# Leaky relu as one parametric relu on ScalarE, and the low weight parts of layers 1 and 2 made on VectorE

## The chip, the cores and the metric

One core of a Trainium2 chip runs the whole program. The metric is the device time of the program in microseconds, lower being better. Its engines are TensorE (PE in the profile, PEld its weight loads), VectorE (DVE), ScalarE (ACT), GpSimd (POOL) and SyncE (SP, which issues the DMAs); 16 DMA engines move the data. Every engine works through its own instructions in the order in which they stand, and waits at the first one whose operands are not ready.

## The reference

A chunked attention over 4 batches of 768 tokens with 8 heads of 64, followed by two MLP blocks over the 3072 tokens, all in float32:

```
scores = scale * (q_c @ k_full.T); scores -= max; a = exp(scores); a /= (sum(a) + 1e-9)
attn   = a @ v_full                       # per chunk of 32 tokens, window of 64 keys
h = x @ w_in;  g = maximum(0.01 * h, h);  x = g @ w_out        # 512 -> 2048 -> 512
a = x @ w_a;   b = x @ w_b;   out = (a * b) @ w_out2           # 512 -> 1536 -> 512
```

## The kernel before

**Products.** A float32 product is made of three passes: each operand is split into a rounded high part (dtype float32r) and a low part, which is the operand minus its high part, and TensorE adds low times high, high times low and high times high. `w_parts` (L91 to L94) does the split of a weight: ScalarE copies it into the high part (L93), another engine subtracts (L94). `split_g` (L316 to L323) does the same for the hidden activations, with L320 on ScalarE and L321 on an engine that is handed in. `a_out` (L289, L290) does it for the output of attention.

**Weights.** They come in as 64 bit words with their halves apart (tile `raw`). For each of the 32 tiles of the first MLP (16 blocks `f` of w_in and 16 of w_out) ScalarE scales the upper half (L79), VectorE joins the two halves with three integer operations (L83, L86, L87) into a tile `z` (three buffers), and then `w_parts` makes the slot `w` that TensorE loads. `Weights.step` joins one tile and splits the one before it. Before the change L94 stands on GpSimd for these 32 tiles.

**Stages.** The tokens go in six blocks `bi` of 512. For each block and each `f`, `mm1` (L377) multiplies x by a block of w_in into a PSUM tile `h` (two buffers), makes the leaky relu and the split, and `mm2` (L388) multiplies the result by a block of w_out and adds into four PSUM tiles; `mm2` is issued two items behind `mm1` (LAG = 2). Block 0 runs while its weights are still being made, in half tiles of 256 tokens, and so has three more items. Beside the items of a block stands the attention of the next four units `u` of 128 tokens: scores on TensorE (L202), softmax on VectorE and ScalarE (L215 to L233, Exp on L220), 16 transposes of `p` into `pt` on VectorE (L246), and the product with v on TensorE (L276). In blocks 1 to 4 the weights of the second MLP are prepared as well (`prep_steps`: `pz`, `ps`, `pw`), their low parts on GpSimd; this part is not changed. After block 5 come layers 3 and 4 (L662 to L740).

**Order.** The kernel is written in one sequence; a scheduling layer then sets the order of each engine's instructions from its own estimate of their durations, so an edit of one instruction moves others too.

**The leaky relu before.** ScalarE makes `t` = 0.01 h out of PSUM (L383), VectorE takes the larger of `t` and `h` (L385), which gives `g`; ScalarE then makes `gh` (L320) and GpSimd (block 0) or VectorE (blocks 1 to 5) makes `gl` (L321). There are 99 such tiles: 93 of 512 columns, 6 of 256.

Of the kernel before, what the change touches and what calls it, by code (L numbers as in the profile page):

```python
# [7 lines left out]
F32 = mybir.dt.float32  # L8
F32R = mybir.dt.float32r
I32 = mybir.dt.int32  # L10
AF = mybir.ActivationFunctionType
ALU = mybir.AluOpType
AX = mybir.AxisListType

P = 128
# [11 lines left out]
TB = 512  # L27
# [4 lines left out]
def kernel(  # L32
# [10 lines left out]
    nc = tc.nc  # L43
# [11 lines left out]
    tp = ctx.enter_context(tc.tile_pool(name="tp", bufs=4, side="right"))  # L55
# [210 lines left out]
    def a_pv(u, pool, tag):  # L266
        pt = PT[u % 2]
        o = pool.tile([P, KC, UT], F32, tag=tag, name="pv")
        for cp in range(2):
            v = vt.pop((u, cp))  # L270
            for pair in range(2):
                for cpar in range(2):
                    for hpar in range(2):
                        i = ((cpar * 2 + hpar) * 2 + pair) * 64
                        t0 = (2 * cp + cpar) * CH
                        nc.tensor.matmul(  # L276
                            o[64 * hpar:64 * hpar + 64, 2 * pair:2 * pair + 2, t0:t0 + CH],
                            v[:, i:i + 64],
                            pt[:, 2 * cp + pair, 2 * cpar + hpar].rearrange("p h q -> p (h q)"),
                            start=True, stop=True,  # L280
                        )
        pvt[u] = o
# [3 lines left out]
    def a_out(u, blk, off):  # L286
        o = pvt.pop(u)
        hi, lo = x1[blk]
        nc.scalar.copy(hi[:, :, off:off + UT], o)  # L289
        nc.vector.tensor_tensor(  # L290
            out=lo[:, :, off:off + UT], in0=o, in1=hi[:, :, off:off + UT].bitcast(F32),
            op=ALU.subtract,
        )

    def x_tiles(key):
        hi = xp.tile([P, KC, TB], F32R, tag="xh", name="xh")
        lo = xp.tile([P, KC, TB], F32R, tag="xl", name="xl")
        x1[key] = (hi, lo)
# [8 lines left out]
    def proj(ps, slot, x, c):  # L307
        hi, lo = x
        for kc in range(KC):
            mm3(  # L310
                ps[:, c],
                (slot[:, 0, kc * P:kc * P + P], slot[:, 1, kc * P:kc * P + P]),
                (hi[:, kc, c], lo[:, kc, c]),
                kc == 0, kc == KC - 1,
            )

    def split_g(g, c, eng):
        gh = tp.tile([P, TB], F32R, tag="gh", name="gh", bufs=3)
        gl = tp.tile([P, TB], F32R, tag="gl", name="gl", bufs=3)
        nc.scalar.copy(gh[:, c], g[:, c])  # L320
        eng.tensor_tensor(  # L321
            out=gl[:, c], in0=g[:, c], in1=gh[:, c].bitcast(F32), op=ALU.subtract
        )  # L323
        return gh, gl
# [6 lines left out]
    W1 = Weights(order)  # L331
# [29 lines left out]
    v_load(6)  # L361
    a_turn_pe(1, ps_a, "a")
    a_out(0, ("x", 0), 0)
    W1.step(nc.gpsimd)
    a_pv(1, ps_h, "h")
    v_load(8)
    W1.load(8)
    W1.split(1, nc.gpsimd)
    a_out(1, ("x", 0), UT)
    a_scores(2)  # L370
    a_soft1(2)
# [5 lines left out]
    def mm1(bi, parts):  # L377
        ps = ps_h.tile([P, TB], F32, tag="h", name="h")
        for o, n, f in parts:
            proj(ps, wslot[f, 0], x1["x", bi], slice(o, o + n))  # L380
        c = slice(min(o for o, _, _ in parts), max(o + n for o, n, _ in parts))
        t = tp.tile([P, TB], F32, tag="t", name="t")
        nc.scalar.mul(t[:, c], ps[:, c], 0.01)  # L383
        g = tp.tile([P, TB], F32, tag="t", name="g")
        nc.vector.tensor_tensor(out=g[:, c], in0=t[:, c], in1=ps[:, c], op=ALU.max)  # L385
        return split_g(g, c, nc.gpsimd if bi == 0 else nc.vector)

    def mm2(bi, parts, g):  # L388
        if bi not in acc:
            acc[bi] = [ps_a.tile([P, TB], F32, tag="a", name="a") for _ in range(KC)]  # L390
        gh, gl = g
        for o, n, f in parts:
            slot = wslot[f, 1]
            t = slice(o, o + n)
            for e in range(KC):
                ps = acc[bi][e][:, t]
                c = slice(e * P, e * P + P)

                kw = dict(skip_group_check=n < TB)
                nc.tensor.matmul(  # L400
                    ps, slot[:, 1, c], gh[:, t], start=f == 0 and o == 0, stop=False, **kw
                )
                nc.tensor.matmul(ps, slot[:, 0, c], gl[:, t], start=False, stop=False, **kw)  # L403
                nc.tensor.matmul(  # L404
                    ps, slot[:, 0, c], gh[:, t], start=False, stop=f == NF1 - 1, **kw
                )
            if f == NF1 - 1:
                for e in range(KC):
                    ps = acc[bi][e][:, t]
                    y = tp.tile([P, TB], F32, tag="z", name="x2", bufs=3)  # L410
                    if e % 2:
                        nc.vector.tensor_copy(y[:, t], ps)  # L412
                    else:
                        nc.scalar.copy(y[:, t], ps)
                    nc.sync.dma_start(out=x2d[bi][:, e, t], in_=y[:, t])
# [114 lines left out]
    def xs_load(sb):  # L530
        for h, tag in enumerate(("xh", "xh" if sb else "xl")):
            t = xp.tile([P, KC, TB], F32, tag=tag, name="xs")
            nc.sync.dma_start(out=t, in_=x2d[2 * sb + h])
            xs[sb, h] = t
# [8 lines left out]
    def xc_make(sb, i):  # L543
        (b11, b21), (b12, b22) = [
            (xs[sb, h][:, 0:HC, :], xs[sb, h][:, HC:KC, :]) for h in range(2)
        ]

        def sub(x, y, key):
            t = xq.tile([P, HC, TB], F32, tag="tt", name="tt", bufs=2)
            nc.vector.tensor_tensor(out=t, in0=x, in1=y, op=ALU.subtract)  # L550
            tt[key] = t
            return t

        if i == 0:
            xc_parts(sb, 0, b11)
            sub(b12, b11, 1)
            sub(b22, tt[1], 2)
        elif i == 1:
            xc_parts(sb, 1, b21)
        elif i == 4:  # L560
            xc_parts(sb, 4, tt[2])
        elif i == 3:
            xc_parts(sb, 3, tt[1])
        elif i == 5:
            xc_parts(sb, 5, sub(b22, b12, 3))
        elif i == 2:
            t = tt[2]
            nc.vector.tensor_tensor(out=t, in0=b21, in1=t, op=ALU.subtract)
            xc_parts(sb, 2, t)
        else:  # L570
            xc_parts(sb, 6, b22)
# [8 lines left out]
    def wo_load(upto):  # L580
        while wo_next[0] < upto:
            b, f = 1 + wo_next[0] // NF1, wo_next[0] % NF1
            if b == NB3:
                break
            t = wop.tile([P, 2, 512], F32R, tag="wo", name="w")
            nc.sync.dma_start(out=t.bitcast(F32), in_=wod[f])
            wslot[f, 1] = t
            wo_next[0] += 1

    for n, (bi, f, parts) in enumerate(items):  # L590
        first, last = bi == 0, bi == NB3 - 1
        if last and f == 0:
            for _ in steps:
                pass
            att.__exit__(None, None, None)
            xq = ctx.enter_context(
                tc.tile_pool(name="xq", bufs=1, side="left", reuse_waits="tile")
            )
        if f == 0 and not last:
            x_tiles(("x", bi + 1))  # L600
        if first:
            W1.load(2 * f + 14)
            W1.step(nc.gpsimd)
        behind.append((bi, parts, mm1(bi, parts)))
        if first:
            W1.step(nc.gpsimd)
        if len(behind) > LAG:
            mm2(*behind.pop(0))
        for fn in beside.get((bi, f), []):
            fn()  # L610
        if not first:
            wo_load((bi - 1) * NF1 + f + 4)

            i = (bi - 1) * NF1 + f
            for _ in range(84 * (i + 1) // 64 - 84 * i // 64):
                next(steps, None)
        elif f >= NF1 - 1:
            wo_load(f - NF1 + 2)
        if last:
            if f == 2:  # L620
                xs_load(0)
            if 4 <= f < 11:
                xc_make(0, CHAIN[f - 4])
# [209 lines left out]
```

## Time and profile before

| | |
|---|---|
| median of 3 runs | 1226.71 us (1224.39 to 1227.79) |
| the profiled execution, its own time | 1226.21 us |
| its span, from the first to the last instruction | 1224.4 us |
| mean granted TensorE clock over the span | 0.982 of full speed |
| PE busy | 1170.7 us, 96% of the span |
| DVE busy | 752.9 us, 61% |
| ACT busy | 383.1 us, 31% |
| POOL busy | 145.4 us, 12% |

Busy shares are averages over stages that have different limits, so they are read together with a table by stage. What a busy engine costs is read from the waits of the engine that sets the end, which here is PE.

### The profile page before, as it was taken

The numbers are of one execution on the slowest core, as the hardware profiler recorded it, in microseconds if no ns is written. First come the engines' busy times: TensorE is split into PE (matmuls) and PEld (weight loads), VectorE is DVE, ScalarE is ACT, GpSimd is POOL, SyncE is SP. The second block draws the span as 40 slices with busy tenths as digits, with TensorE's granted clock in tenths as the row PEclk, the third lists the DMA queues.
The fourth block names the chain that finished last, engine by engine and source line by source line (L and its number), as shares of the span: only waits on it lengthen the run. The fifth ranks groups of instructions, "written<-read, shape, count | busy, mean of one in ns | idle before, by whom it ended". The sixth has DMA issues, their size and how long they took to land.

```text
span 1224.4 us, 16825 instructions
## 1 busy us (share of the span) xinstructions
PE 1170.7 (96%) x6632; PEld 984.1 (80%) x6632; DVE 752.9 (61%) x1313; ACT 383.1 (31%) x642; POOL 145.4 (12%) x109
## 2 busy tenths in 40 slices
PE   5788799989998999999999999999999999999998
PEld 5778788867887887888888888888888888888887
DVE  5999959795897899666622443447443447433443
ACT  3634333243334433222422222224122223222220
POOL 1544512032122222000000000000000000000000
PEclk9898999989999999999999999999999999999999
DMA  9766658768887887642633843537453535453512
GB/s 322 256 229 194 210 186 306 268 238 299 297 304 254 310 311 261 212 138 86 221 106 108 319 158 120 193 125 280 162 215 130 198 131 208 158 204 120 189 61 103
DMA packets 63822, 250.72 MB, mean 205 GB/s; under 512 B 7424, under 2 KB 8832, under 8 KB 56832
## 3 DMA queue, kind: packets, MB, share of 16 engines
q1 hardware_dynamic: 63744, 249.66, 57.5%
q8 instruction: 52, 0.85, 0.3%
q14 instruction: 26, 0.21, 0.1%
HBM read 200.34 MB, written 49.28 MB: 204 GB/s over the span
## 4 chain that ended last, share of the span: by engine, by line
PE 67%; DVE 2%; DMA 1%; issue 0%; POOL 0%; SPq 0%; DVEq 0%; POOLq 0%
PE o L729 5%; PE o L730 5%; PE o L731 5%; PE A L662 4%; PE A L663 4%; PE A L664 4%; PE h L303 4%; PE a L403 4%; PE a L404 4%; PE a L400 4%; PE h L304 3%; PE h L305 3%; PE C L662 3%; PE C L663 3%; PE C L664 3%; PE D L663 1%
## 5 line engine op out<-in xcount | busy, mean ns | idle before, releaser
L303 PE MATMUL h<-xh,w 128*128 128x512 f32 (+1 forms) x448 | 168.8, 377 | 17.5 <-POOL w L94 14.7
L400 PE MATMUL a<-gh,w 128*128 128x512 f32 (+1 forms) x448 | 161.3, 360 | 4.8 <-DVE x L412 2.3
L304 PE MATMUL h<-xl,w 128*128 128x512 f32 (+1 forms) x448 | 164.2, 367 | 0.5 <-DVE xl L290 0.5
L305 PE MATMUL h<-xh,w 128*128 128x512 f32 (+1 forms) x448 | 163.7, 365 | 0.0
L403 PE MATMUL a<-gl,w 128*128 128x512 f32 (+1 forms) x448 | 160.8, 359 | 0.0
L404 PE MATMUL a<-gh,w 128*128 128x512 f32 (+1 forms) x448 | 160.8, 359 | 0.0
L303 PEld LDWEIGHTS h<-xh,w 128*128 128x128 f32 x448 | 87.5, 195 | 33.2 <-POOL w L94 15.7
L729 PE MATMUL o<-w,cl 128*128 128x512 f32 x288 | 112.1, 389 | 0.2 <-DMA w<-wod 0.2
L730 PE MATMUL o<-w,ch 128*128 128x512 f32 x288 | 112.0, 389 | 0.0
L731 PE MATMUL o<-w,ch 128*128 128x512 f32 x288 | 112.0, 389 | 0.0
L385 DVE TENSOR_TENSOR g<-t,h 128x512 f32<-128x512 f32 (+1 forms) x99 | 66.1, 668 | 67.3 <-ACT t L383 66.5
L320 ACT CAST gh<-g 128x512 fp32r<-128x512 f32 (+1 forms) x99 | 60.1, 607 | 149.5 <-DVE g L385 144.1
L246 DVE STREAM_TRANSPOSE pt<-p 32x128 f32<-32x128 f32 x320 | 96.8, 302 | 5.5
L400 PEld LDWEIGHTS a<-gh,w 128*128 128x128 f32 x448 | 84.6, 189 | 18.6 <-DVE x L412 2.9
L304 PEld LDWEIGHTS h<-xl,w 128*128 128x128 f32 x448 | 87.7, 196 | 13.1 <-DVE xl L290 0.9
L305 PEld LDWEIGHTS h<-xh,w 128*128 128x128 f32 x448 | 87.0, 194 | 13.3
L404 PEld LDWEIGHTS a<-gh,w 128*128 128x128 f32 x448 | 84.7, 189 | 12.5
L403 PEld LDWEIGHTS a<-gl,w 128*128 128x128 f32 x448 | 84.6, 189 | 12.5
L383 ACT ACTIVATE t<-h 128x512 f32<-128x512 f32 (+1 forms) x99 | 57.5, 581 | 110.3 <-PE h L305 110.3
L684 DVE TENSOR_TENSOR ga<-u,C 128x512 f32<-128x512 f32 x36 | 24.8, 688 | 105.4 <-ACT u L676 76.2
L676 ACT COPY u<-A 128x512 f32<-128x512 f32 x72 | 42.3, 587 | 143.5 <-PE A L664 143.5
L662 PE MATMUL A<-ch,wab 128*128 128x512 f32 x216 | 84.1, 389 | 0.0
(95 smaller groups left out, 2116.3 us busy)
## 6 DMA issues: line engine op xcount, KB each, us to landing
wab<-wab SPq DMA_DIRECT2D x36, 1792.0 KB, 7.3
w<-wod SPq DMA_DIRECT2D x116, 512.0 KB, 4.7
raw<-w SPq DMA_DIRECT2D x68, 512.0 KB, 5.9
wab<-pw SPq DMA_DIRECT2D x12, 1792.0 KB, 6.7
k<-kl SPq DMA_DIRECT2D x48, 256.0 KB, 4.3
v<-vl SPq DMA_DIRECT2D x48, 256.0 KB, 4.7
wod<-w SPq DMA_DIRECT2D x16, 512.0 KB, 5.3
q<-ql SPq DMA_DIRECT2D x48, 128.0 KB, 4.1
```

What stands on the lines that cost most here:

```text
L246: nc.vector.transpose(out=pt[o0:o0 + 32, :, 2 * cpar + hpar, hpx, :], in_=p[i0:i0 + 32, hpx::2, 32 * b:32 * b + 32],)
L303: nc.tensor.matmul(ps, w[1], x[0], start=first, stop=False)
L304: nc.tensor.matmul(ps, w[0], x[1], start=False, stop=False)
L305: nc.tensor.matmul(ps, w[0], x[0], start=False, stop=last)
L400: nc.tensor.matmul(ps, slot[:, 1, c], gh[:, t], start=f == 0 and o == 0, stop=False, **kw)
L403: nc.tensor.matmul(ps, slot[:, 0, c], gl[:, t], start=False, stop=False, **kw)
L404: nc.tensor.matmul(ps, slot[:, 0, c], gh[:, t], start=False, stop=f == NF1 - 1, **kw)
L662: nc.tensor.matmul(ps, w[:, 1, i, c], hi[:, kc], start=first and kc == 0, stop=False, **kw)
L663: nc.tensor.matmul(ps, w[:, 0, i, c], lo[:, kc], start=False, stop=False, **kw)
L729: nc.tensor.matmul(o, cl[:, q], w[:, 0, :], start=k == 0, stop=False)
L730: nc.tensor.matmul(o, ch[:, q], w[:, 1, :], start=False, stop=False)
L731: nc.tensor.matmul(o, ch[:, q], w[:, 0, :], start=False, stop=k == NCH - 1)
```

## The change

The two instructions on L383 and L385 become one on ScalarE, a parametric relu with slope 0.01 that reads `h` in PSUM and writes `g`; the tile `t` is gone. `W1.step` and `W1.split` are called with VectorE in place of GpSimd, so L94 of the 32 weight tiles of the first MLP moves there. GpSimd keeps L321 of block 0 and the preparation of the second MLP's weights. In the changed kernel the lines behind L383 stand two lines higher.

```diff
@@ before block 0
-    W1.step(nc.gpsimd)
+    W1.step(nc.vector)
     a_pv(1, ps_h, "h")
     v_load(8)
     W1.load(8)
-    W1.split(1, nc.gpsimd)
+    W1.split(1, nc.vector)
@@ mm1
-        t = tp.tile([P, TB], F32, tag="t", name="t")
-        nc.scalar.mul(t[:, c], ps[:, c], 0.01)
         g = tp.tile([P, TB], F32, tag="t", name="g")
-        nc.vector.tensor_tensor(out=g[:, c], in0=t[:, c], in1=ps[:, c], op=ALU.max)
+        nc.scalar.activation(g[:, c], ps[:, c], AF.Prelu, alpha=0.01)
         return split_g(g, c, nc.gpsimd if bi == 0 else nc.vector)
@@ the items of block 0
         if first:
             W1.load(2 * f + 14)
-            W1.step(nc.gpsimd)
+            W1.step(nc.vector)
         behind.append((bi, parts, mm1(bi, parts)))
         if first:
-            W1.step(nc.gpsimd)
+            W1.step(nc.vector)
```

The scheduling layer also moves what stands around these instructions. The first place is VectorE's order in the middle of block 0, where the weights are joined (L83, L86, L87 write a `z`, whose number is the same in the row of its L94). Before:

```order
L86 SCALAR_TENSOR_TENSOR z_652<-raw_357,z_652 128x512
L83 TENSOR_SCALAR z_677<-raw_359 128x512
L87 SCALAR_TENSOR_TENSOR z_652<-raw_357,z_652 128x512
L86 SCALAR_TENSOR_TENSOR z_677<-raw_359,z_677 128x512
L83 TENSOR_SCALAR z_718<-raw_361 128x512
L87 SCALAR_TENSOR_TENSOR z_677<-raw_359,z_677 128x512
L86 SCALAR_TENSOR_TENSOR z_718<-raw_361,z_718 128x512
L385 TENSOR_TENSOR g_712<-t_710,h_685 128x512
L87 SCALAR_TENSOR_TENSOR z_718<-raw_361,z_718 128x512
```

The same place in the changed kernel:

```order
L86 SCALAR_TENSOR_TENSOR z_708<-raw_361,z_708 128x512
L94 TENSOR_TENSOR w_713<-z_669,w_713 128x512
L87 SCALAR_TENSOR_TENSOR z_708<-raw_361,z_708 128x512
L86 SCALAR_TENSOR_TENSOR z_733<-raw_363,z_733 128x512
L83 TENSOR_SCALAR z_772<-raw_365 128x512
L87 SCALAR_TENSOR_TENSOR z_733<-raw_363,z_733 128x512
L94 TENSOR_TENSOR w_738<-z_708,w_738 128x512
L86 SCALAR_TENSOR_TENSOR z_772<-raw_365,z_772 128x512
L94 TENSOR_TENSOR w_777<-z_733,w_777 128x512
```

The maximum is gone, and one L94 stands in for each tile; between the last operation on a `z` (its L87) and its L94 stand two or three other instructions here, and two to five at most other places.

The second place is VectorE's order in block 1 at the transposes of unit 11, for which TensorE's L276 waits. Before:

```order
L233 TENSOR_TENSOR p<-p,l 128x512
L492 TENSOR_TENSOR ps<-pz 128x256
L246 STREAM_TRANSPOSE pt_139<-p 32x4x32 x4
L385 TENSOR_TENSOR g<-t,h 128x512
L246 STREAM_TRANSPOSE pt_139<-p 32x4x32 x4
L321 TENSOR_TENSOR gl<-g,gh 128x512
L246 STREAM_TRANSPOSE pt_139<-p 32x4x32 x8
L493 TENSOR_TENSOR ps<-pz,ps 128x256
```

The same place in the changed kernel:

```order
L231 TENSOR_SCALAR l<-l 128x8
L232 RECIPROCAL l<-l 128x8
L233 TENSOR_TENSOR p<-p,l 128x512
L246 STREAM_TRANSPOSE pt_139<-p 32x4x32 x16
L321 TENSOR_TENSOR gl<-g,gh 128x512
L83 TENSOR_SCALAR pz<-raw 128x512
```

The maximum and the L321 that stood between the transposes are out of the train of 16. TensorE's own order stays as it was but for a few neighbouring rows in block 0, and SyncE's does so up to the end of block 0.

## Rows read from the trace of the kernel before

**Rows 1.** The page, part 1: busy time of each engine over the span.

```profile
PE 1170.7 (96%) x6632; PEld 984.1 (80%) x6632; DVE 752.9 (61%) x1313; ACT 383.1 (31%) x642; POOL 145.4 (12%) x109
```

**Rows 2.** Busy time by stretch: from:to, length, engines, granted clock, DMA share, GB/s.

```profile
20.00:175.00 155.00, 126.51 (x1158) 120.48 (x1157) 134.78 (x224) 65.81 (x121) 68.84 (x51) 0.90 0.67 226
175.00:660.00 485.00, 472.06 (x2852) 390.20 (x2851) 356.29 (x703) 172.06 (x286) 73.39 (x48) 0.99 0.67 236
...
900.00:1100.00 200.00, 200.00 (x884) 165.67 (x883) 90.34 (x131) 52.09 (x84) 0.00 (x0) 1.00 0.48 178
```

**Rows 3.** PE's waits, 20 to 165 us: us in total, times, longest.

```profile
PE h L303 <- POOL w L94: 14.7, 6, 5.8
PE pv L276 <- DVE pt L246: 9.0, 9, 1.7
```

**Rows 4.** PE's waits, 165 to 660 us.

```profile
PE pv L276 <- DVE pt L246: 9.5, 7, 2.7
PE a L400 <- DVE x L412: 2.3, 1, 2.3
PE h L303 <- DVE g L385: 0.7, 1, 0.7
```

**Rows 5.** DVE's groups by shape, 20 to 165 us: busy us, mean ns | idle before.

```profile
L87 DVE SCALAR_TENSOR_TENSOR z<-raw,z 128x512 int32<-128x512 int32 x31 | 33.0, 1067 | 0.3
L86 DVE SCALAR_TENSOR_TENSOR z<-raw,z 128x512 int32<-128x512 int32 x31 | 29.7, 960 | 0.3
L83 DVE TENSOR_SCALAR z<-raw 128x512 int32<-128x512 int32 x31 | 21.2, 686 | 2.6 <-ACT raw L79 1.3 <-issue 1.3
...
L385 DVE TENSOR_TENSOR g<-t,h 128x512 f32<-128x512 f32 x13 | 8.8, 679 | 0.1
L233 DVE TENSOR_TENSOR p<-p,l 128x512 f32<-128x512 f32 x6 | 6.3, 1051 | 0.1
...
L385 DVE TENSOR_TENSOR g<-t,h 128x256 f32<-128x256 f32 x5 | 2.1, 417 | 1.3 <-ACT t L383 1.3
```

**Rows 6.** Timeline of DVE, then of POOL, at 86 us: start, duration.

```profile
85.97 0.68 DVE L86 SCALAR_TENSOR_TENSOR z<-raw,z 128x512 int32<-128x512 int32 x1
86.57 0.42 DVE L83 TENSOR_SCALAR z<-raw 128x512 int32<-128x512 int32 x1
86.91 1.76 DVE L87 SCALAR_TENSOR_TENSOR z<-raw,z 128x512 int32<-128x512 int32 x1
...
86.84 1.28 POOL L321 TENSOR_TENSOR gl<-g,gh 128x512 fp32r<-128x512 f32 x1 [5.84 <-DMA raw<-w]
```

**Rows 7.** Groups by shape over the span, of DVE and of ACT.

```profile
L94 DVE TENSOR_TENSOR cl<-gb,ch 128x512 fp32r<-128x512 f32 x72 | 49.7, 692 | 33.1 <-ACT ch L93 29.9
...
L383 ACT ACTIVATE t<-h 128x512 f32<-128x512 f32 x93 | 55.2, 594 | 104.9 <-PE h L305 104.9
...
L220 ACT ACTIVATE p<-p 128x512 f32<-128x512 f32 x24 | 15.1, 631 | 47.0 <-DVE p L217 47.0
L220 ACT ACT_TABLE_LOAD x1 | 1.3, 1283 | 0.7 <-PEq L815 0.7
```

**Rows 8.** Timeline of DVE, then of PE, at the transposes of unit 11.

```profile
261.19 1.24 DVE L246 STREAM_TRANSPOSE pt<-p 32x128 f32<-32x128 f32 x4
262.46 0.69 DVE L385 TENSOR_TENSOR g<-t,h 128x512 f32<-128x512 f32 x1
...
264.46 1.75 DVE L321 TENSOR_TENSOR gl<-g,gh 128x512 fp32r<-128x512 f32 x1
266.22 2.54 DVE L246 STREAM_TRANSPOSE pt<-p 32x128 f32<-32x128 f32 x8
...
267.52 0.47 PE L276 MATMUL pv<-pt,v 128*64 128x64 f32 x2 [2.71 <-DVE pt L246]
```

**Rows 9.** Waits over the span, of POOL and of DVE, for ScalarE's casts.

```profile
POOL w L94 <- ACT w L93: 62.2, 21, 16.2
...
DVE cl L94 <- ACT ch L93: 34.5, 38, 2.9
```

## The prediction

> **What bounds the kernel now.** I read the page's busy shares first. PE is busy for 1170.7 of 1224.4 us [rows 1], so nothing that the change does to DVE, ACT or POOL counts unless it takes away a time in which PE stands still or runs slowly; 53.7 us is all that PE stood. The second view is the table by stretch [rows 2]. The reader should see that behind 660 us there is nothing to win: the row from 900 to 1100 has PE busy for 200.00 of 200.00 us at full clock. What is lost lies ahead of that, in two stages. From 20 to 175 us (block 0, while its weights are made) PE is busy for 126.5 of 155 us, with a mean granted clock of 0.90; DVE is busy for 134.8 of the 155, more than PE. From 175 to 660 us (blocks 1 to 4, and 5) PE stands for 485 - 472 = 13 us at clock 0.99, and DVE is busy for 356 of 485.
>
> The third view, PE's waits, says for whom. In block 0 it is the weights' low parts that GpSimd makes on L94, 14.7 us, and DVE's transposes, 9.0 us [rows 3]. Later it is the transposes again, 9.5 us, and two DVE operations with 2.3 and 0.7 us [rows 4]. Both stages so wait for DVE's queue, the first partly by way of POOL. The change works on just that: it takes work from DVE everywhere and puts other work on it in block 0.
>
> **The maximum, L385.** The 99 DVE instructions go. In block 0 that is 8.8 + 2.1 = 10.9 us of a nearly full DVE [rows 5]; in the later blocks it is 93 - 13 = 80 of the 0.68 us kind [rows 5, 7], 54 us of DVE time. The pass on ACT stays one pass: L383 took 594 ns as a multiplication out of PSUM [rows 7]. The price of a parametric relu is in no row. Its nearest rows are L383 itself (594 ns) below and Exp with 631 ns above [rows 7]; I take 631, which adds 99 x 0.04 = 4 us to an ACT that is busy for 31% [rows 1], and I cost that at nothing. If it took twice L383, ACT would hold 59 us more, still under half of the span, and `mm2` stands two items behind, so that price is not an end of the range. The chain from `h` to `gh` also loses a handover to DVE, and the buffer of `h` comes free one instruction earlier, which is the 0.7 us wait of [rows 4].
>
> **L94 on DVE.** It adds 32 instructions in block 0. The same operation and shape on DVE took 692 ns [rows 7], so 32 x 0.692 = 22.1 us.
>
> **What POOL took from DVE.** The third part is not in the diff. L86 took 0.68 us at 85.97, and L87 of the same kind took 1.76 us at 86.91, just while POOL ran an instruction from 86.84 on [rows 6]. So DVE's integer operations are held while POOL works. Without that they take 0.68, 0.68 and 0.42 us (L87, L86, L83); their means in block 0 are 1.067, 0.960 and 0.686 [rows 5]. That is 31 x (0.387 + 0.280 + 0.266) = 28.9 us, and L233 adds 6 x (1.051 - 0.692) = 2.2 us, together 31.1 us over the 51 POOL instructions of the stretch [rows 2], 0.61 us for each. The 32 that leave POOL give back 32 x 0.61 = 19.5 us; the 19 L321 that stay keep theirs.
>
> On this the Trainium skill is sharper: "SBUF — State Buffer", section "SBUF: two separate sides", calls the port pair of VectorE and GpSimd an exclusive lock that one instruction holds for its whole length while the other engine fully blocks. By that rule each moved instruction gives back a whole block. The trace agrees for a single instruction, 1.76 against 0.68 us, but its mean is 0.61 us, and I go by the mean.
>
> **The new wait.** L94 needs ScalarE's cast of the same tile (L93), so DVE now waits in order for ACT, and the joins and transposes behind it wait too. Nothing shows that price for these tiles on DVE. From below it is nothing: the cast is a pass over 512 columns like L383's 594 ns [rows 7], and two or three DVE instructions of 0.4 to 0.7 us [rows 6] stand between the last join of a tile and its L94 where the order is shown, up to seven elsewhere. From above I take DVE's L94 in the later layers, which waited 34.5 us over 93 instructions, 0.37 us each [rows 9]: 32 x 0.37 = 11.9 us. I take 4 us, a third, as most places have the cover.
>
> **Block 0, the sum.** DVE: -10.9 + 22.1 - 19.5 + 4 = -4.3 us. PE, which waits for DVE there, gains that. Beside it the last step to a weight is shorter, 0.69 us where a POOL subtraction took 1.28 us [rows 6], and each wait that gets shorter costs less of the clock behind it (0.90 on average [rows 2], so up to 12 us in all). I give these two together 2 us: block 0 is worth -6 us. Its ends are -21 us (the lock at its full price, below) and +4 us (the wait at its full price).
>
> **Blocks 1 to 4, the sum.** At unit 11 the 16 transposes took from 261.19 to 268.8 us, 7.6 us for what is 16 x 0.31 = 5.0 us, since a maximum and an L321 of 1.75 us stand between them [rows 8]; PE waited there, 2.71 us at once. In the changed order the 16 stand together, and some 3 maxima per unit ahead of them are gone as well (2 us). That is more than PE's longest wait. So I take the transposes' 9.5 us and the 0.7 us as gone [rows 4], keep the 2.3 us for L412, and add 1 us of the clock (0.99 over 472 us is some 5 us). Sum: -11 us. Its ends are 0 (something else is late at the same places) and -18 us (all of the 13 us and the clock).
>
> **Forecast.** -6 - 11 = -17 us on the profiled execution's 1226.2 us gives 1209 us. That execution stands 0.5 us under the median of the runs, which changes nothing here. What one can tell from no change is about 0.3%, 3.7 us: under 1223.0 is faster, over 1230.4 slower.
>
> **Rivals.**
> - *The full lock.* Each moved POOL instruction gives back 1.76 - 0.68 = 1.08 us, 34.6 us in place of 19.5. DVE's sum in block 0 falls by another 15 us, and the time comes out at 1194 us. For it speaks the single instruction of [rows 6]; against it the mean, since POOL often runs beside transposes or PSUM reads, which it seems not to hold (L385, which reads PSUM, has a mean of 0.68 us in block 0 [rows 5]). This is the skill's rule of the lock taken at its word.
> - *The wait at its full price.* L94 waits 0.37 us each: DVE in block 0 comes out at -4.3 - 4 + 11.9 = +3.6 us, and the later gain stays: 1226.2 + 3.6 - 11 = 1219 us.
> - *No gain.* PE's order is almost unchanged, and where one wait ends another may stand behind it (the data of `v`, the cast of `pv`, ACT's chain). PE has several waits per place in [rows 3], which speaks for it; that DVE was busy for longer than PE in block 0 [rows 2] speaks against. Time: 1225 us.
> - *Slower: DVE stands where POOL stood.* POOL's L94 waited for ACT 62.2 us in 21 waits, 2.96 us each [rows 9], which cost nothing on an idle engine. On DVE, with some 1.9 us of other work between, 1.06 us would be left at each of 32: 34 us. Then block 0 is at -4.3 - 4 + 34 = +26, the total at +15, the time at 1241 us. The point from which this decides: all gains together are 8.3 + 11 = 19.3 us, so a mean stall of 0.60 us per L94. Against it: POOL waited so long because it had nothing else to do.
> - *Slower: two tables.* If Exp and the parametric relu needed different tables, each of the 22 Exps behind the first relu would bring two loads of 1.283 us [rows 7], 56 us in the attention's chain, hence 1226 - 17 + 56 = 1265 us. The order of the changed program has one load, as before. The Trainium skill, "ScalarE: Activation LUTs", section "Table sets: the hidden batching unit", is where such a change of set is described; the trace of before has a single load and can't show it.
>
> **How the numbers follow.** Forecast 0.52 (its own range 1202 to 1216), full lock 0.13, wait at full price 0.17: faster 0.82. No gain: 0.09. DVE stands 0.07, two tables 0.02: slower 0.09. The range reaches from 1193, with the full lock's 1194 inside, to 1226, with half of the no-gain case; outside lie the slower cases, some of no gain, and part of the full lock where the clock comes back too, under 0.2.
>
> **What would show it.** In the changed profile: no L385; ACT's L383 near 0.6 us, one table load; DVE's L94 on `w` 32 times near 0.69 us, with under 6 us of waits for ACT; the means of L86 and L87 in block 0 down from about 1.0 to about 0.8 us; DVE's busy time down by 66 - 22 + 20, some 64 us, or more; PE's waits for `w` at half of 14.7 us or less; PE's waits for transposes behind 165 us at 1 us or so, and transposes in trains of 5 us. The forecast is wrong if PE's waits in block 0 come back with DVE's L94 as their releaser, or if the means of L86 and L87 stay near 1 us.

## The result, and the profile after

The changed kernel takes 1191.26 us (median of 4 runs, 1190.74 to 1194.71) against 1226.52 us for the kernel before on the same chip; the ratio is 0.972, 95% interval 0.9697 to 0.9743. Predicted were 1209 us and a range from 1193 to 1226: the direction was right and the gain twice the forecast. The profiled execution is the slowest of the four, 1194.71 us, 31.5 us under that of before; the working below is made against it.

The page of the changed kernel, part 1 (before: [rows 1]):

```profile
PE 1158.3 (97%) x6632; PEld 974.7 (82%) x6632; DVE 681.2 (57%) x1246; ACT 383.2 (32%) x642; POOL 109.6 (9%) x77
```

Busy time by stretch, with the columns of [rows 2] and the same stretches:

```profile
20.00:175.00 155.00, 140.17 (x1273) 132.74 (x1271) 129.58 (x268) 75.97 (x139) 38.68 (x22) 0.96 0.78 267
175.00:660.00 485.00, 477.90 (x2869) 394.86 (x2869) 297.41 (x605) 168.38 (x279) 67.74 (x45) 0.99 0.68 238
900.00:1100.00 200.00, 200.00 (x884) 165.64 (x884) 89.41 (x129) 52.11 (x85) 0.00 (x0) 1.00 0.46 170
```

PE is busy for 140 of the 155 us from 20 to 175 instead of 126.5, at a mean clock of 0.96 instead of 0.90; the last 23 us of that stretch now belong to block 1. Behind 660 us nothing has changed.

PE's waits over the whole span (us in total, times, longest), of which [rows 3, 4] show before:

```profile
PE a L398 <- DVE x L410: 7.1, 4, 3.3
PE s L202 <- DMA k<-kl: 6.5, 2, 5.1
PE h L303 <- DVE w L94: 5.5, 2, 5.4
PE a L401 <- POOL gl L321: 5.3, 1, 5.3
PE pv L276 <- DVE pt L246: 2.8, 5, 1.0
```

The 14.7 us for GpSimd's `w` have become 5.5 us for VectorE's, nearly all in one wait at the very start of block 0 (5.4 us up to 30.7; the same wait took 5.8 us before). The transposes' 18.5 us are down to 2.8. New are 5.3 us for the one `gl` that GpSimd was late with, and a larger wait for the evictions of the accumulators (L410, which stood on L412 before: 2.3 us).

VectorE's groups by shape, 20 to 165 us (busy us, mean ns | idle before), which answer to [rows 5]:

```profile
L94 DVE TENSOR_TENSOR w<-z,w 128x512 fp32r<-128x512 f32 x32 | 23.0, 720 | 0.6 <-ACT w L93 0.4
L86 DVE SCALAR_TENSOR_TENSOR z<-raw,z 128x512 int32<-128x512 int32 x31 | 22.0, 712 | 0.0
L87 DVE SCALAR_TENSOR_TENSOR z<-raw,z 128x512 int32<-128x512 int32 x31 | 21.9, 706 | 0.0
...
L83 DVE TENSOR_SCALAR z<-raw 128x512 int32<-128x512 int32 x31 | 14.0, 460 | 0.1
...
L233 DVE TENSOR_TENSOR p<-p,l 128x512 f32<-128x512 f32 x6 | 4.1, 683 | 0.0
...
L231 DVE TENSOR_SCALAR l<-l 128x8 f32<-128x8 f32 x6 | 1.0, 163 | 0.0
```

The last of them, L231, before:

```profile
L231 DVE TENSOR_SCALAR l<-l 128x8 f32<-128x8 f32 x6 | 3.2, 528 | 0.0
```

This is the main reading. L87 fell from 1067 to 706 ns, L86 from 960 to 712, L83 from 686 to 460, L233 from 1051 to 683: together 11.1 + 7.7 + 7.2 + 2.2 = 28.2 us came back, of the 31.1 us that the prediction had counted as held by GpSimd. A fifth group that it had not looked at, L231 (8 columns), fell from 3.2 to 1.0 us: in all 30.4 us.

ScalarE's groups over the span (before: [rows 7]):

```profile
L383 ACT ACTIVATE g<-h 128x512 f32<-128x512 f32 x93 | 55.2, 593 | 149.7 <-PE h L305 149.7
...
L220 ACT ACT_TABLE_LOAD x1 | 1.3, 1283 | 0.7 <-PEq L813 0.7
```

A parametric relu out of PSUM costs what the multiplication cost, 593 ns, and needs no second table.

To say where the time came from I use two marks in every trace: the time at which PE has been given 196,000 of the columns of `mm1` and `mm2` (block 0 has 196,608), and 1,170,000 (all six blocks have 1,179,648). "Block 0" in the table is the first mark, "later part" the time between the two. Behind the second mark every kernel takes 547 to 549 us more.

| kernel | median us | ratio to before (95%) | block 0 us | later part us |
|---|---|---|---|---|
| before | 1226.52 | | 172.8 | 503.9 |
| after | 1191.26 | 0.972 (0.9697 to 0.9743) | 152.1 | 493.3 |
| e1 relu alone | 1197.31 | 0.9769 (0.9747 to 0.9791) | 165.2 | 482.9 |
| e2 low parts alone | 1200.35 | 0.9789 (0.9766 to 0.9811) | 159.6 | 492.0 |
| e3 gl on VectorE too | 1186.59 | 0.9684 (0.9659 to 0.9709) | 147.9 | 489.0 |
| e4 e3, GpSimd kept busy | 1196.37 | 0.9761 (0.9735 to 0.9788) | 158.1 | 490.2 |
| e5 relu in blocks 1 to 5 only | 1210.29 | 0.9883 (0.9867 to 0.99) | 170.9 | 492.4 |
| e6 e3, evictions on ScalarE | 1183.36 | 0.9671 (0.965 to 0.9692) | 147.8 | 484.8 |
| e7 first three gl on VectorE | 1186.99 | 0.9694 (0.9679 to 0.9709) | 146.2 | 489.6 |
| e10 maximum back in blocks 1 to 5 | 1203.19 | 0.9818 (0.9801 to 0.9835) | 152.5 | 501.5 |

The ratios are each against runs of before in the same session. From before to after block 0 gained 20.7 us (forecast 6) and the later part 10.6 us (forecast 11).

### The profile page after: what moved, and what is told of

Same layout as the page of the kernel before. It is cut to its first block, busy times and chain, and to the rows that moved or that the text cites. A ratio compares the mean times of both kernels' runs of the same rounds, so it can differ in the third digit from the quotient of the medians.

```text
span 1192.9 us, 16632 instructions
## 1 busy us (share of the span) xinstructions
PE 1158.3 (97%) x6632; PEld 974.7 (82%) x6632; DVE 681.2 (57%) x1246; ACT 383.2 (32%) x642; POOL 109.6 (9%) x77
## 4 chain that ended last, share of the span: by engine, by line
PE 81%; DVE 10%; DMA 3%; POOL 2%; issue 2%; ACT 1%; SPq 0%; DVEq 0%; ACTq 0%; POOLq 0%
PE o L727 5%; PE o L729 5%; PE o L728 5%; PE h L303 5%; PE a L398 5%; PE a L401 5%; PE a L402 5%; PE h L304 5%; PE h L305 5%; PE A L660 4%; PE A L662 4%; PE A L661 4%; PE C L660 3%; PE C L662 3%; PE C L661 3%; PE s L202 3%
## 5 line engine op out<-in xcount | busy, mean ns | idle before, releaser
L303 PE MATMUL h<-xh,w 128*128 128x512 f32 (+1 forms) x448 | 165.2, 369 | 5.5 <-DVE w L94 5.5
L304 PE MATMUL h<-xl,w 128*128 128x512 f32 (+1 forms) x448 | 161.8, 361 | 0.0
L305 PE MATMUL h<-xh,w 128*128 128x512 f32 (+1 forms) x448 | 161.7, 361 | 0.0
L402 PE MATMUL a<-gh,w 128*128 128x512 f32 (+1 forms) x448 | 161.6, 361 | 0.0
L321 DVE TENSOR_TENSOR gl<-g,gh 128x512 fp32r<-128x512 f32 x80 | 61.9, 776 | 102.2 <-ACT gh L320 101.5
L383 ACT ACTIVATE g<-h 128x512 f32<-128x512 f32 (+1 forms) x99 | 57.5, 580 | 157.1 <-PE h L305 157.1
L303 PEld LDWEIGHTS h<-xh,w 128*128 128x128 f32 x448 | 85.1, 190 | 19.5 <-issue 5.8
L305 PEld LDWEIGHTS h<-xh,w 128*128 128x128 f32 x448 | 85.1, 190 | 13.0
L304 PEld LDWEIGHTS h<-xl,w 128*128 128x128 f32 x448 | 85.3, 190 | 12.0
L661 PE MATMUL A<-cl,wab 128*128 128x512 f32 x216 | 84.1, 389 | 0.0
```

The lines of the kernel that those rows point to most:

```text
L303: nc.tensor.matmul(ps, w[1], x[0], start=first, stop=False)
L304: nc.tensor.matmul(ps, w[0], x[1], start=False, stop=False)
L305: nc.tensor.matmul(ps, w[0], x[0], start=False, stop=last)
L402: nc.tensor.matmul(ps, slot[:, 0, c], gh[:, t], start=False, stop=f == NF1 - 1, **kw)
L661: nc.tensor.matmul(ps, w[:, 0, i, c], lo[:, kc], start=False, stop=False, **kw)
```

## The experiments

**The two parts apart, e1 and e2.** In e1 the low parts stay on GpSimd; in e2 the maximum stays.

```diff
-    W1.step(nc.vector)       # e1: at all four places, split too
+    W1.step(nc.gpsimd)
```

> The parametric relu alone; the low weight parts stay on GpSimd. Theory T (the gain in block 0 is VectorE's time there: 11 us for the maximum, about 7 us net for the low parts and the port that GpSimd leaves; the gain of about 10 us in blocks 1 to 4 is the maximum alone): block 0 about 10 us shorter than before, the later blocks about 10 us shorter, some 1206 us; means of L86 and L87 on VectorE stay near 1 us. Theory R (block 0 gains by the shorter way to a weight, so by the low parts alone): only the later 10 us, some 1216 us.

```diff
-        nc.scalar.activation(g[:, c], ps[:, c], AF.Prelu, alpha=0.01)   # e2
+        t = tp.tile([P, TB], F32, tag="t", name="t")
+        nc.scalar.mul(t[:, c], ps[:, c], 0.01)
+        nc.vector.tensor_tensor(out=g[:, c], in0=t[:, c], in1=ps[:, c], op=ALU.max)
```

> The low weight parts on VectorE alone; the leaky relu stays in two steps. Theory T: block 0 some 7 to 10 us shorter, the later blocks unchanged with their 9.5 us of waits for transposes, some 1218 us; means of L86 and L87 in block 0 down to 0.75 us. Theory R: all of the 21 us of block 0, some 1205 us.

Both came out faster than any of these numbers, and the two gains (27.5 and 24.4 us against the 1224.77 us of that session) add up to more than both together bring. The table by stage says where. In block 0 they add: 7.6 + 13.2 = 20.8 us, and the changed kernel gained 20.7. In the later part they don't (21.0, 11.9, and 10.6 together). The groups of e1, 20 to 155.5 us, and of e2, 20 to 153.2 us (each to the last transpose of unit 7):

```profile
L87 DVE SCALAR_TENSOR_TENSOR z<-raw,z 128x512 int32<-128x512 int32 x31 | 31.7, 1026 | 0.4
L86 DVE SCALAR_TENSOR_TENSOR z<-raw,z 128x512 int32<-128x512 int32 x31 | 29.6, 958 | 0.7
L83 DVE TENSOR_SCALAR z<-raw 128x512 int32<-128x512 int32 x31 | 21.0, 679 | 6.6 <-ACT raw L79 5.8 <-issue 0.7
```

```profile
L86 DVE SCALAR_TENSOR_TENSOR z<-raw,z 128x512 int32<-128x512 int32 x31 | 27.5, 887 | 0.0
L94 DVE TENSOR_TENSOR w<-z,w 128x512 fp32r<-128x512 f32 x32 | 22.9, 716 | 0.2
L87 DVE SCALAR_TENSOR_TENSOR z<-raw,z 128x512 int32<-128x512 int32 x31 | 21.9, 707 | 0.0
...
L83 DVE TENSOR_SCALAR z<-raw 128x512 int32<-128x512 int32 x31 | 14.7, 479 | 0.1
```

With the low parts on GpSimd (e1) the three joins stay near 1 us; with them on VectorE (e2) L87 and L83 are nearly free. L86 is not: in e2 it is held by `gl`, which is still on GpSimd. I went through the timelines and counted VectorE's joins, L94 and softmax instructions (L231, L233) in block 0 that took over 0.15 us more than undisturbed, with the GpSimd instruction that each overlapped. Before: 35 of them, 33.1 us, 25 beside an L94 of `w` (23.4 us) and 10 beside an L321 (9.7 us). In e2: 15, 12.0 us, all beside L321. After: 6, 4.4 us. So the L94 were the costly ones, 0.94 us where they hit; and what an L321 costs is not fixed, since the same 19 cost 9.7, 12.0 or 4.4 us as their neighbours change.

Theory R falls, since block 0 gained in both. Theory T's sizes for block 0 (10 us, and 7 to 10) were off both ways. In e1 VectorE now waited 5.8 us for ScalarE's scaling of `raw` (L83's row; 1.3 us in [rows 5]). In e2 VectorE's time alone does not explain the 13.2 us: its holds fell by 21.1 us, but L94 added 22.9; its last transpose of unit 7 still came 8.4 us earlier (153.2 instead of 161.6), and the mean clock up to there was 0.96 instead of 0.90. How much of the rest is the shorter way to a weight, no run separates.

**No GpSimd in block 0, e3, and GpSimd busy for nothing, e4.**

```diff
-        return split_g(g, c, nc.gpsimd if bi == 0 else nc.vector)   # e3, e4
+        return split_g(g, c, nc.vector)
```

```diff
+                nc.gpsimd.tensor_tensor(   # e4, for each weight tile; nothing reads junk
+                    out=junk, in0=w[:, 0, 0:344].bitcast(F32), in1=w[:, 0, 0:344].bitcast(F32),
+                    op=ALU.subtract,
+                )
```

> The changed kernel with gl of block 0 (L321) on VectorE too, so that GpSimd has no work in block 0. Theory T (GpSimd's L321 stood still for 11 us while VectorE ran back to back, and PE's 5.3 us wait for it is that): that wait is gone, no VectorE operation in block 0 is held, VectorE has 11.5 - 4.4 = 7 us more; PE had slack against VectorE in block 0 only at some places, so between 1187 and 1194 us. Rival (VectorE's load alone sets the end of block 0): 7 us more than the changed kernel, 1198 us.

> The kernel of the run before with one more instruction on GpSimd for each of the 32 weight tiles, which subtracts 344 columns of the high part from themselves into a tile that nobody reads: GpSimd's use of the port without anyone waiting for it. Theory A (a GpSimd instruction of this chain costs VectorE what it cost before, 23.4 us over 32): VectorE's L86 and L87 back to 0.9 us or more, VectorE 15 to 23 us busier in block 0, and the time 12 to 20 us over that run. Theory B (VectorE keeps the port while its operations stand back to back, as for L321 in the changed kernel, 0.23 us each): VectorE 7 us busier or less, GpSimd's instructions long, the time 0 to 6 us over that run.

e3 is faster than the changed kernel, by 4.7 us, just past the lower edge of what the theory expected. All holds are gone: L86, L87, L83 and L94 take 681, 679, 421 and 685 ns. e4 then puts GpSimd work back that nobody waits for and that is on no chain: 1196.37 us, 9.8 us more, and block 0 is 10.2 us longer. VectorE's and ScalarE's instructions in block 0 stand in the same order in e3 and e4. Busy time up to the last transpose of unit 7, with the columns of [rows 2], in e3 and in e4:

```profile
20.00:141.10 121.10, 111.70 (x1079) 107.10 (x1077) 115.69 (x251) 65.09 (x117) 0.00 (x0) 0.97 0.83 284
20.00:149.90 129.90, 114.01 (x1069) 107.98 (x1069) 125.54 (x250) 64.93 (x116) 49.70 (x32) 0.96 0.77 260
```

VectorE is busy for 9.9 us more with the same instructions. That isolates the cause: GpSimd's mere running costs block 0 time by way of VectorE. The size lay between the two expectations: counted as above, and with `gl`, which now is VectorE's too, 21 instructions were held for 10.5 us, 0.33 us for each of the 32 on GpSimd. These took 0.76 us at the least, but six took 1.9 to 2.5 us and one 14.15, since they did not get in between (see e7 and e11).

**The port by itself, e8.** All of the kernel's work is left out. VectorE runs trains of one kind of instruction, alone and then beside five GpSimd subtractions of 512 columns. Of this probe and the two below there is one execution each.

```diff
+    for f in (two, sub, one, psum, copy, turn):   # L73, L79, L83, L89, L93, L97
+        pool()                                    # five subtractions on GpSimd, L69
+        f(40 if f is turn else 14)
```

> No part of the computation is left: only VectorE's kinds of instruction in trains, first alone, then each train (14 instructions, 40 for the transposes) beside five GpSimd subtractions of 512 columns out of SBUF. Theory K (the hold depends on the kind: an instruction that reads two operands from SBUF is held, one that reads one operand, or PSUM, is not, which is why an equal share of 0.61 us for each GpSimd instruction was too low for L94, which ran beside the joins): the two-operand trains take 5 x 0.9 to 5 x 1.1 us, about 5 us, longer in all, or keep GpSimd out to their end; the trains out of PSUM and of transposes take the same time as alone within 0.05 us an instruction. Rival E (every kind is held alike, and the mean is low because GpSimd often met a VectorE that stood): all trains are longer by 3 to 5 us.

The probe's timeline (start, duration): trains of 6 (12 transposes) alone, GpSimd's five alone, then pairs.

```profile
6.70 4.31 DVE L73 SCALAR_TENSOR_TENSOR zo<-zj,zi 128x512 int32<-128x512 int32 x6
17.54 2.72 DVE L83 TENSOR_SCALAR zo<-zi 128x512 int32<-128x512 int32 x6
21.42 4.29 DVE L89 TENSOR_TENSOR zo<-za,ps 128x512 f32<-128x512 f32 x6
32.23 3.97 DVE L97 STREAM_TRANSPOSE zo<-za 32x128 f32<-32x128 f32 x12
37.40 6.62 POOL L69 TENSOR_TENSOR po<-pa,ph 128x512 f32<-128x512 f32 x5 [0.27 <-DVE za L100]
44.81 14.83 DVE L73 SCALAR_TENSOR_TENSOR zo<-zj,zi 128x512 int32<-128x512 int32 x14
44.98 8.31 POOL L69 TENSOR_TENSOR po<-pa,ph 128x512 f32<-128x512 f32 x5 [0.27 <-DVE za L109]
76.70 11.11 DVE L83 TENSOR_SCALAR zo<-zi 128x512 int32<-128x512 int32 x14
88.98 10.06 DVE L89 TENSOR_TENSOR zo<-za,ps 128x512 f32<-128x512 f32 x14
111.36 13.30 DVE L97 STREAM_TRANSPOSE zo<-za 32x128 f32<-32x128 f32 x40
```

Two operands out of SBUF: 14 x 0.718 = 10.05 us alone, 14.83 beside, so 0.96 us for each GpSimd instruction. The tensor_scalar (L83's kind): 14 x 0.453 = 6.35 us alone, 11.11 beside, again 0.95. One of the two operands out of PSUM: 10.01 and 10.06, nothing; transposes: 40 x 0.331 = 13.2 and 13.30, nothing. Theory K holds, but for the tensor_scalar, which reads one operand and is held all the same. The Trainium skill, "SBUF — State Buffer", section "SBUF: two separate sides", has the lock taken by instructions with two SBUF inputs and by those in a mode that uses both ports, against GpSimd. That the two-operand instructions are held and the transposes are not agrees with it; the tensor_scalar would agree if it runs in such a mode, which no run here shows (it takes 0.42 us where those of two operands take 0.68).

**Can GpSimd be kept out? e7, e9, e11.** In the changed kernel one `gl` of block 0 took 12.62 us. GpSimd's timeline there, the wait of PE behind it, VectorE's last instruction before it ran dry, and the stretches behind:

```profile
46.70 12.62 POOL L321 TENSOR_TENSOR gl<-g,gh 128x512 fp32r<-128x512 f32 x1 [3.78 <-ACT gh L320]
```

```profile
59.37 0.58 PE L401 MATMUL a<-gl,w 128*128 128x256 f32 x1 [5.34 <-POOL gl L321]
```

```profile
57.52 0.68 DVE L86 SCALAR_TENSOR_TENSOR z<-raw,z 128x512 int32<-128x512 int32 x1
```

```profile
55.00:60.00 5.00, 0.63 (x3) 0.63 (x4) 3.20 (x7) 2.44 (x5) 5.00 (x2) 0.63 1.04 419
60.00:65.00 5.00, 5.00 (x42) 4.86 (x41) 0.00 (x0) 0.00 (x0) 1.78 (x2) 0.69 0.86 350
```

Its operand was ready at 46.7. VectorE ran joins and L94 without a gap from 46.13 to 58.20, and `gl` was done 1.1 us after VectorE stopped; VectorE's next instruction, L215, waited for scores from PE, and PE stood for that very `gl`. PE then ran for 5 us at a mean granted clock of 0.69, so for part of them at the lower of its two levels, 1.2 GHz. e7 makes the first three `gl` (256 columns each) on VectorE and leaves 16 on GpSimd:

```diff
-        return split_g(g, c, nc.gpsimd if bi == 0 else nc.vector)
+        return split_g(g, c, nc.gpsimd if bi == 0 and parts[0][2] > 2 else nc.vector)
```

> The changed kernel with gl of block 0's first three half items (256 columns each) on VectorE, the other 16 still on GpSimd. Theory W (of what all of gl on VectorE gains, nearly all is the one wait of 5.3 us for the first gl, which GpSimd could not make while VectorE ran without a gap): that wait goes, 1186 to 1188 us, though the holds of VectorE by the other gl (4.4 us) stay. Rival H (the gain is those holds): 1190 to 1192 us.

Theory W: 1186.99 us, as good as e3. The wait for `gl` is gone. Of the 16 that stay on GpSimd 6 hold VectorE, for 5.1 us, and the time is still that of e3, where VectorE makes them all; so rival H falls. e9 and e11 look for the keeping out itself, in trains that write three tiles in turn, so that VectorE's instructions start 0.60 us apart as in block 0.

> No part of the computation is left: again trains of VectorE instructions beside five GpSimd subtractions, but each train (18 instructions) now writes three tiles in turn, so that no instruction has to wait for the end of the one before it; in the first probe all wrote one tile and started 0.72 us apart, where those of block 0 start 0.60 us apart. Theory G (GpSimd comes in between two VectorE instructions only where VectorE leaves a gap): beside the trains of subtractions, of integer operations and of the mix, the first GpSimd subtraction lasts until the train ends, 18 x 0.60 = 10.8 us, and the train itself is not stretched; in the train with a copy out of PSUM at every fourth place GpSimd comes in at the first copy, after some 2 to 3 us. Rival T (what kept GpSimd's first gl out for 12.6 us in the changed kernel is something else): GpSimd's subtractions take about 1.7 us each, as in the first probe, and each stretches the train by 0.95 us.

> No part of the computation is left: trains of 24 VectorE instructions without gaps again, but GpSimd's first subtraction now waits for a chain of ScalarE copies, so that it becomes ready some 3 us behind the start of the train, as gl becomes ready in the middle of VectorE's work in block 0; in four sections the chain ends 0.1 us or so later each time, and in the fifth a copy out of PSUM stands in the middle of the train. In the second probe both started together and then took turns. Theory Q (a GpSimd instruction that becomes ready while VectorE runs without a gap comes in only at a gap or at an instruction that does not need the port): the first subtraction lasts until the train ends, 24 x 0.60 = 14.4 us less the 3 us before it, so 8 to 12 us, and in the fifth section until the copy, under 5 us; VectorE's train is not stretched before that. Rival T2 (they take turns then too): the first subtraction takes 1.3 to 2.0 us in all sections, and VectorE's next instruction 1.75 us; what held gl for 12.6 us in the changed kernel then stays open.

In e9 theory G fell: GpSimd and VectorE took turns in every train without PSUM, one instruction each, the mix with the tensor_scalar included; each turn held VectorE for 1.07 us (1.75 instead of 0.68, 1.48 instead of 0.41). The trains of e11 are those of e9, but GpSimd's instruction becomes ready in the middle. GpSimd in its first, fifth and sixth section, and the copy out of PSUM in the fifth:

```profile
13.17 1.68 POOL L115 TENSOR_TENSOR po<-pa,ga 128x512 f32<-128x512 f32 x1 [4.03 <-DVE zr L74]
```

```profile
86.11 3.42 POOL L115 TENSOR_TENSOR po<-pa,ga 128x512 f32<-128x512 f32 x1 [4.11 <-ACT ga L113]
```

```profile
88.33 0.68 DVE L87 COPY zo<-ps 128x512 f32<-128x512 f32 x1
```

```profile
102.07 9.58 POOL L115 TENSOR_TENSOR po<-pa,ga 128x512 f32<-128x512 f32 x1 [4.10 <-ACT ga L113]
```

In four trains of two-operand instructions alone GpSimd got its turn at once (1.28 to 1.68 us). In the two trains that also have tensor_scalar instructions it did not: in the sixth it waited until VectorE's train had ended, in the fifth until the copy out of PSUM, after which it needed its usual time; in neither was VectorE held before that. So theory Q holds in these two sections and T2 in the other four. Their mix is that of block 0, and there too each long wait of GpSimd ended with a gap of VectorE or an instruction out of PSUM: in e7 one `gl` took 5.82 us, up to a gap of 0.15 us; in e2 one took 4.72 us, up to a maximum (L385), which reads PSUM; the 14.15 us in e4 ended with a gap of 0.21 us. But the mix alone doesn't decide. In e9, where both engines started together, it took turns, and in the kernel before, beside the same joins, no GpSimd instruction of block 0 took over 1.75 us. What decides is not settled.

**The later part, e5, e6, e10.** e5 is the kernel before with the relu in blocks 1 to 5 only; e10 is the changed kernel with the maximum back there.

```diff
-        if bi == 0:      # e5: the maximum on VectorE in block 0, the relu elsewhere
+        if bi > 0:       # e10: the other way round, low parts on VectorE
```

> The kernel before with the parametric relu in blocks 1 to 5 only; block 0 keeps the maximum on VectorE, and the low parts of the weights stay on GpSimd. Theory S (the maximum in the later blocks is what costs the waits there): block 0's work ends near 173 us as before, and the later part falls from 503.9 us to about 483 us, as with the relu everywhere, so about 1225 - 21 = 1204 us. Rival O (what the later part gains depends on how the order and the loads happen to fall, not on its own maxima): the later part falls by 10 us or less, 1214 us or more.

> The changed kernel with the maximum back on VectorE in blocks 1 to 5 only; block 0 has the parametric relu, and the low parts of the weights are on VectorE. Theory M (what the later part gained, about 11 us, is the maxima that left VectorE there): block 0 ends near 152 us, the later part is back at 500 to 504 us, 1200 us or more in all. Rival P (the waits of the later part in the kernel before depend on how transposes, evictions and late loads happen to meet, and go whichever part of the program is changed; the kernel with the maxima and the low parts on VectorE had 492 us there): the later part is 490 to 494 us, 1190 to 1194 us in all.

Taking the later maxima out of the kernel before shortens its later part by 503.9 - 492.4 = 11.5 us (between the two expectations, nearer rival O's); putting them back into the changed kernel lengthens it by 501.5 - 493.3 = 8.2 us, and the time by 11.9 us (theory M). PE's waits there, 155 to 650 us of the changed kernel, and 160 to 655 us of e10 and of e2:

```profile
PE a L398 <- DVE x L410: 6.3, 3, 3.3
PE a L398 <- ACT x L412: 0.4, 1, 0.4
PE pv L276 <- DVE pt L246: 0.4, 2, 0.2
```

```profile
PE pv L276 <- DVE pt L246: 4.9, 5, 2.7
PE h L303 <- ACT xh L289: 3.5, 1, 3.5
PE a L404 <- DVE x L416: 2.9, 2, 2.1
PE h L303 <- DVE g L387: 0.7, 1, 0.7
```

```profile
PE a L400 <- DVE x L412: 3.5, 3, 2.1
PE pv L276 <- DVE pt L246: 1.9, 3, 1.0
PE a L403 <- DVE gl L321: 0.9, 1, 0.9
```

So two pairs agree on 8 to 12 us, with the transposes' wait as what goes. But e2, which changes nothing behind block 0, gained 11.9 us there too, and e1 lost no time at all to waits there (482.9 us): part of that wait seems to hang on where block 0 leaves the engines, which no run isolates, and one can't read a single kernel's later part to a few us. What remained after the change were the evictions, which stand in VectorE's queue behind the preparation of later weights. e6 puts all four on ScalarE:

```diff
-                    if e % 2:
-                        nc.vector.tensor_copy(y[:, t], ps)
-                    else:
-                        nc.scalar.copy(y[:, t], ps)
+                    nc.scalar.copy(y[:, t], ps)
```

> The kernel with all of gl on VectorE, and with all four evictions of the accumulators at a block's end on ScalarE (before: two on VectorE). Theory V (what is still lost in the later part is VectorE's eviction, queued behind the preparation of weights that waits for a late load): TensorE's waits for L410, 3.4 us, go, and the clock behind them too; the later part falls from 489 to about 483 us, 1181 us in all. Rival A (ScalarE stands behind the same late load): its evictions are waited for in their place, 1186 us or more.

The waits for evictions behind block 0, in e3 and in e6:

```profile
PE a L398 <- DVE x L410: 3.4, 1, 3.4
```

```profile
PE a L398 <- ACT x L409: 1.4, 1, 1.4
```

VectorE's 3.4 us are gone, ScalarE's 1.4 us are what is left of the wait, and the later part is down from 489.0 to 484.8 us. Theory V is nearer. With 1183.36 us this is the fastest kernel of the study, though its interval still overlaps that of e3.

## Why the prediction was right and wrong

**Block 0 is where it failed, and the step is "What POOL took from DVE".** It shared 31.1 us evenly over the 51 GpSimd instructions of the stretch, 0.61 us each, gave 32 shares back (19.5 us) and let "the 19 L321 that stay keep theirs" (11.6 us). Measured: 28.2 us of the 31.1 came back, and 30.4 with L231, 10.9 us more than forecast. The even share was too low for L94. An L94 of `w` runs just when VectorE joins the next tile, and the joins are of the kinds that are held; 25 of the 32 held an instruction, for 0.94 us each, near the probe's 0.96, which makes 23.4 us in place of 19.5. The larger part of the miss is that the 19 L321 did not keep theirs: 10 of them held an instruction before, for 9.7 us, and 6 after, for 4.4 us. Their neighbours had changed: in the changed kernel seven stood beside transposes (three before), three beside a VectorE without work, and one was itself kept out. For L94 the evidence was in the rows: the single instruction of [rows 6] showed 1.08 us, and the probe has 1.07; what the mean of 0.61 lacked was a look at which GpSimd instruction stood beside each long join. That L321 would meet other instructions no row could show; the prediction took its neighbours as fixed and gave no reason.

**The new wait** was the other miss, in the same direction: L94 waited 0.4 us for ScalarE's cast, not 4. The rule "two or three instructions stand between" was enough cover; the upper bound from the later layers had no bearing here.

The sum, up to the last transpose of unit 7, by groups: -10.0 (maximum; two tiles of 256 columns of [rows 5] come behind that point) + 23.0 (L94; 22.1 was forecast) - 30.4 + 0.4 = -17.0 us for VectorE, where -4.3 stood. The stretches themselves, before and after:

```profile
20.00:161.60 141.60, 114.63 (x1064) 109.66 (x1062) 131.43 (x217) 62.16 (x111) 66.64 (x48) 0.90 0.70 237
20.00:143.90 123.90, 109.58 (x1063) 106.26 (x1060) 110.93 (x233) 63.33 (x116) 32.92 (x18) 0.94 0.78 267
```

VectorE's point moved by 17.7 us: its busy time fell by 20.5 (back to back its instructions start 0.60 us apart, so an L94 adds less than its 0.72), its idle time rose by 2.8. PE's mark moved by 20.7; the 2 us for the shorter path and the clock were, at 3.0, not far off, though the late `gl` took some of it back (in e7, without it, block 0 is 5.9 us shorter still).

**The later part came out as forecast, partly by luck**: -11 forecast, -10.6 measured, the waits for transposes gone (0.4 us left) and the 16 transposes in one train (5.1 us at 235.9). The eviction's 2.3 us, which I kept, grew to 6.3, and the clock made up for it: against e1's 482.9 us without a wait, before lost 21.0 us, 13.0 of it in waits of PE, and after 10.4 us, 7.1 of it in waits; so the clock behind the waits gave back 8.0 - 3.3 = 4.7 us where I had put 1 (between the marks PE is busy for 490.95 us before, 486.29 after and 482.86 in e1, for the same work). As e1 and e2 show, the agreement is better than the reasoning behind it deserves.

**The relu** at 593 ns and one table: the bound from below held, and the rival of two tables fell. The rivals of a slower kernel fell too; VectorE did take GpSimd's place without a wait.

**The rival that came nearest was the full lock**: 1194 us, against 1194.7 for the profiled execution. Its hold of 1.08 us is right; its number is so in part by luck. It counts 34.6 us for the 32 that moved, as if each had held an instruction, and they had held 23.4 us in all; what L321 no longer held, and the wait of 4 us that was 0.4, made up most of the rest. I gave it 0.13 because of the mean. The range's low end, 1193, lay just under it, and the median, 3.4 us below the profiled execution, fell outside.

**Of the signs named**: no L385, one table load, 32 L94 at 0.72 us with 0.4 us of waits, DVE's busy time down by 71.7 us (64 or more), waits for `w` down to 5.5 (under half of 14.7), transposes in trains: all as named. L86 and L87 at 0.71 instead of 0.8 us is the sign that shows the failed step.

## What to carry to other kernels

When GpSimd and VectorE work side by side, don't price GpSimd by a mean over its instructions: list which VectorE instruction stands beside each, charge about one hold (here 1 us for 1.3 us of GpSimd) for those that read two SBUF operands and for a tensor_scalar like L83, and nothing for those out of PSUM or for transposes. List it for the GpSimd work that stays, too, since its neighbours change. Moving such work to a VectorE that is already the bound can shorten VectorE's queue, here by 30.4 us for 23.0 us of added work. A GpSimd result that TensorE needs soon can be kept out by a stretch of VectorE without gaps.

## What the runs showed that was not expected

- GpSimd can be kept out for many VectorE instructions: 12.62 us for one `gl` in the changed kernel, 14.15 us for one subtraction in e4 and 9.58 us in the probe, each until VectorE stopped, or in e11's fifth section until an instruction out of PSUM came (3.42 us).
- An instruction of 8 columns is held as well: L231 took 528 ns on average before and 163 ns after.
- GpSimd work that nothing waits for made the kernel 9.8 us slower (e4).
- GpSimd's low parts for the second MLP hold VectorE in the later blocks too: counted in the same way, 21 instructions for 25 us between 175 and 660 us of the changed kernel (before: 25 for 28 us). The L321 of 1.75 us in [rows 8] is one of them: GpSimd's L94 of `pw` runs from 264.39 us. No run takes this work off GpSimd.
